# Made w2 sets in three tied parts from raw slots of their own, and probabilities transposed two positions later (tiles 9 to 17)

## The chip, the cores and the metric

One core of a Trainium2 chip runs the whole program in one launch. The metric is the device time of that core in microseconds. The kernel before took 1995.99 us, the median of three runs (1995.85 to 1996.73).

## The reference

Three layers follow one another. 2304 tokens of width 512 come out of an attention with a window of 64 keys; they go through a gated layer, and then through eight experts that all see every token and are added with weights from a normalisation of eight rounds.

```
scores = scale * q @ k.T ; masked to 0 <= rel < 64 ; softmax ; attn @ v     (4 x 8 heads, 576 x 64)
x = attn_out reshaped to 2304 x 512
x = (silu(x @ w_gate) * (x @ w_val)) @ w_out                                 (512 -> 1536 -> 512)
P = exp(x @ r_gate - max) ; 8 rounds of row and column normalisation         (2304 x 8)
out = sum over e of P[:, e] * (relu(x @ w1[e]) @ w2[e])                       (512 -> 1024 -> 512, e = 0..7)
```

## The kernel before, in words

The program has three stretches. First the attention of the first four tiles of 128 tokens. Then the gated layer, in five blocks of 4, 4, 4, 4 and 2 tiles, with the attention of the later tiles woven in. Last the experts. Products are made of a high and a low part of each operand, so each product is three passes: high by high, high by low, low by high.

The middle stretch is a list of events that is walked once (`ev`, `add`). Its unit is a position: twelve matmuls of 512 columns. Three positions make one hidden tile f of block b: "gv" kind 0 (gate, PSUM bank 4), "gv" kind 1 (value, bank 5) and "o" (the output product of the hidden tile before, banks 0 to 3). Position 3s+kind belongs to hidden tile s = 12b+f. Around these, the stages of attention tile t are put at p plus an offset, with p = 9(t-5) for t from 4 on (`STEPS`, `SHIFT`): transposes of q and k ("tqk", L297, banks 4 and 7), scores ("s", L320, banks 6 and 7, reduced by VectorE at L332), exponentials on ScalarE ("exp", L409), the normalisation on VectorE ("norm", L417 to L423), transposes of the probabilities ("t", L440, banks 6 and 7, copied out by ScalarE at L282 and VectorE at L284), and the product with v ("pv", L457, bank 6, copied out by ScalarE at L470 and VectorE at L473). At three positions after each block's end the router's logits of that block are made ("lg", L826, bank 6; copied at L841) and transposed ("lgt", L853, bank 7). A scheduler then sets each engine's order from these events; an engine works through its list in that order and does not pass over an instruction that waits.

ScalarE and VectorE also split weights into high and low parts. `split_1` does it for the gated layer (L605 on ScalarE, L606 on VectorE; from "saved" copies in DRAM). `split_w2q` makes one set of w2 of an expert: it reads two raw tiles, forms sums and differences (L700, L701, L715, L716), splits seven pieces (L675, L678 on ScalarE, L684, L687 on VectorE) into a staging buffer of seven tiles, and stores them in one DMA of 1792 KB (L731) for the experts' stretch. There are 20 such sets (experts 1 to 5, four each), two in every three hidden tiles from s = 12 on, each as one event.

All raw tiles, saved weights and w2 alike, come through one ring of slots (`o_raw` of six, and two more, `o_more`, in the middle stretch: `place_raws`), in the order in which they are used. A load is issued by SyncE when its slot's last reader is done (`load_one`, L560). All DMAs of the program are issued by SyncE, in one list.

Of the kernel before, what the change touches and what calls it, by code (L numbers as in the profile page):

```python
# [17 lines left out]
def attention_moe_moe2(  # L18
# [13 lines left out]
    nc = tc.nc  # L32
# [63 lines left out]
    o_ident = take("F", 128)  # L96
    o_ones = take("F", 128)
    o_mask = take("F", 3 * WK)
    o_logit = take("F", NTILE * NE)
    o_prob = take("F", NTILE * NE)  # L100
    o_rows = take("F", NTILE)
    o_cols = take("F", NE)
    o_part = take("F", NE)
    o_gmax = take("F", 2)
    o_stat = take("F", NSC * 3 * H)
    o_lgs = takes("F", 128, 6)
    o_wgp = take("F", KD * 32)
    NRAW = 6
# [11 lines left out]
    o_acc = takes("F", 512, 2 * HTT)  # L120
    o_more = o_acc[4:6]
    sizes["F"] = max(sizes["F"], f_top)
# [4 lines left out]
    o_qraw = takes("bF", 512, 3)  # L127
    o_kraw = takes("bF", 512, 3)
    o_xc = take("bR", 2 * 7 * 2 * HT)

# [16 lines left out]
    o_wc = [o_x[1], o_wr[4], o_x[0]]  # L147
    o_stw = [o_w2[0], o_w2[4]]

    o_last = take("R", 2 * HT)  # L150
# [56 lines left out]
    def emit_consts():  # L207
        make_identity(nc, ident)
        nc.vector.tensor_copy(sl(o_idr, 128, True), ident)
        m = sl(o_stage + 512, 192)  # L210
        nc.gpsimd.memset(m, 0.0)

        nc.gpsimd.affine_select(out=m, in_=m, pattern=[[1, 192]], compare_op=ALU.is_gt, fill=NEG, base=0, channel_multiplier=-1)
        nc.gpsimd.affine_select(out=m, in_=m, pattern=[[-1, 192]], compare_op=ALU.is_ge, fill=NEG, base=WIN, channel_multiplier=1)

        for i in range(3):
            for r, c, n in ((0, 64, 64), (0, 0, 64), (64, 64, WK)):
                rows = slice(r, r + 64)
# [8 lines left out]
        nc.gpsimd.memset(ones, 1.0)  # L227
        nc.gpsimd.memset(sl(o_wgp, KD * 32), 0.0)
# [290 lines left out]

    raw_at = []  # L520
    raw_prev = []
    raw_done = set()
    raw_held = set()

    def place_raws(ready):
        ring = o_raw + o_more
        last = {}
        for n in range(len(raw_keys)):
            if n < 2 * NCONV:
                o = o_raw[n % NRAW]  # L530
            elif n < ready:
                o = ring[(n - 2 * NCONV) % len(ring)]
            else:
                o = next(raw_at[i] for i in range(n - len(ring), n) if raw_at[i] in o_raw and last[raw_at[i]] == i)
            raw_at.append(o)
            raw_prev.append(last.get(o))
            last[o] = n

# [6 lines left out]
    def load_one():  # L545
        n = w_load[0]
        if n >= raw_stop[0] or n >= 2 * NCONV and raw_prev[n] is not None and raw_prev[n] not in raw_done:
            return False
        w_load[0] += 1
        key, i = raw_keys[n]  # L550
        src = sources(key)[i]
        if wide(key):
            dst = sl(o_wide[n % NWIDE], 1024).bitcast(I32)
        elif key[0] == "x":
            dst = sl(raw_at[n], HT)
        else:
            dst = sl(raw_at[n], 512)
# [50 lines left out]
    def raw_slots(key):  # L608
        cnt = sum(1 for r in raw_keys if r[0] == key)
        n = w_next[0]  # L610
        assert raw_keys[n][0] == key and w_load[0] >= n + cnt, (key, n, w_load)
        w_next[0] += cnt
        return [raw_at[n + i] for i in range(cnt)]

# [119 lines left out]

# [40 lines left out]
    def do_split(key):  # L775
        {"1": split_1, "w1": split_w1, "w2": split_w2, "w2q": split_w2q, "x": split_x}[key[0]](key)

# [80 lines left out]

    def emit_gmax1():
        nc.vector.tensor_reduce(sl(o_gmax, 1), logit, AX.X, ALU.max)  # L860
        nc.vector.tensor_copy(sl(o_lgs[0], 128), sl(o_gmax, 1).to_broadcast([128, 128]))
# [459 lines left out]
    def add(*e):  # L1321
        ev.append(e)
# [143 lines left out]
    }  # L1466
    made = [("w2q", e, 0, j) for e in range(1, NE - 2) for j in range(NF2 // 2)]
    seq = [(b, f) for b in range(NB) for f in range(NF1)]
    prev = None
    for s, (b, f) in enumerate(seq):  # L1470
        for kind in range(3):
# [12 lines left out]
            att_at(3 * s + kind)  # L1484
        if s == 1:
# [7 lines left out]
    assert not made  # L1493
    late = [("w1", 0, 0, 2), ("w2", 0, 0, 6), ("w1", 0, 0, 3), ("w2", 0, 0, 7)]
# [87 lines left out]

    raw_first = []
    for e in ev:
# [7 lines left out]
        elif e[0] == "w2h" and e[3] == 0:  # L1592
            key = ("w2q", e[1], 0, e[2])
        if e[0] == "w1n" and key is not None and not raw_first:
            raw_first.append(len(raw_keys))
        if key is not None:
            raw_keys.extend((key, i) for i in range(len(sources(key))))

    place_raws(raw_first[0])

# [21 lines left out]
    def banks(x):  # L1622
# [45 lines left out]
        "unlock": emit_unlock,  # L1668
        "w2h": emit_w2h,
        "w2r": emit_w2r,  # L1670
        "p": emit_p,
# [13 lines left out]
    for e in ev:  # L1685
# [6 lines left out]
        if e == ("gv", NB - 1, NF1 - 1, 1):  # L1692
            last_hid.update((ins.engine, ins) for ins in added[begin:])
        if e[0] == "w2h":
            for ins in added[begin:]:
                if ins.engine in (mybir.EngineType.DVE, mybir.EngineType.Activation):
                    tc.add_manual_dep(
# [44 lines left out]
```

## Time and profile before

| | |
|---|---|
| median of three runs | 1995.99 us |
| the profiled execution | 1994.68 us |
| its span, first to last instruction | 1992.9 us |
| TensorE (matmul) busy | 1965.0 us, 99% |
| VectorE busy | 1509.4 us, 76% |
| ScalarE busy | 1233.9 us, 62% |
| GpSimd busy | 41.2 us, 2% |
| DMA: moved, mean rate | 529.36 MB, 266 GB/s |

Busy time is the time in which an engine has an instruction of the program running. Matmuls overlap and their ends are modelled. A busy TensorE is one that has work, not one at its peak. What an engine waits for is inferred from the semaphores. The profiled execution took 1.8 us more than its span, which lies before the first and after the last instruction.

### The profile page before, as it was taken

To read this page: it belongs to the slowest core of one execution; us is meant where nothing else is said; L and a number is where in the kernel's file an instruction comes from. 1 tells how busy PE (TensorE), PEld (TensorE's weight loads), DVE (VectorE), ACT (ScalarE), POOL (GpSimd) and SP (SyncE) were. 2 spreads that over 40 slices of the span, in tenths; PEclk is the share of its full clock that TensorE was granted. 3 is DMA by queue.
4 is the path that set the end of the run, shared out by engine and by line. 5 is a ranking of instruction groups with operands and counts; after the bars stand their busy time and mean duration, and the time that the engine had idled before them with its cause. 6 is when DMAs were issued, how large, how long until landed. Compare 5 with 4: busy or idle time off the path is not lost.

```text
span 1992.9 us, 33648 instructions
## 1 busy us (share of the span) xinstructions
PE 1965.0 (99%) x11815; PEld 1855.9 (93%) x11815; DVE 1509.4 (76%) x3298; ACT 1233.9 (62%) x2795; POOL 41.2 (2%) x77
## 2 busy tenths in 40 slices
PE   8999999999999999999999999999999999999998
PEld 6887877778998999999999999999999999999998
DVE  7987777877677999989987777868777566666566
ACT  7766676766552677777764566657565455555555
POOL 3100000000000000000000000000000000000000
PEclk9999999999999999999999999999999999999999
DMA  9988889777764869979888889989877877777775
GB/s 243 280 271 253 247 230 290 240 242 222 230 225 166 302 212 296 369 244 342 264 287 268 262 301 325 333 301 333 289 248 267 279 260 261 261 260 246 268 240 170
DMA packets 303002, 529.36 MB, mean 266 GB/s; under 512 B 74976, under 2 KB 159728, under 8 KB 302320
## 3 DMA queue, kind: packets, MB, share of 16 engines
q1 hardware_dynamic: 302832, 527.21, 81.2%
q8 instruction: 93, 1.52, 0.3%
q14 instruction: 77, 0.63, 0.1%
HBM read 390.74 MB, written 136.39 MB: 265 GB/s over the span
## 4 chain that ended last, share of the span: by engine, by line
PE 91%; DVE 3%; DMA 3%; ACT 2%; issue 0%; SPq 0%; POOL 0%; DVEq 0%; ACTq 0%
PE ps L1138 34%; PE ps L1271 34%; PE ps L788 12%; PE ps L806 6%; DMA area_F<-in_moe_w_dram 2%; PE ps L965 2%; PE ps L919 2%; PE ps L457 1%; PE ps L440 1%; ACT area_bF L409 0%; PE ps L297 0%; PE ps L320 0%; PE ps L1301 0%; DVE area_R L606 0%; DVE area_bF L423 0%
## 5 line engine op out<-in xcount | busy, mean ns | idle before, releaser
L1138 PE MATMUL ps<-area_bR,area_R 128*128 128x384 f32 x3864 | 771.5, 335 | 0.0
L1271 PE MATMUL ps<-area_R 128*128 128x384 f32 x3864 | 770.6, 334 | 0.0
L1138 PEld LDWEIGHTS ps<-area_bR,area_R 128*128 128x128 f32 x3864 | 678.0, 188 | 1.6 <-ACT area_F L1306 0.3
L1271 PEld LDWEIGHTS ps<-area_R 128*128 128x128 f32 x3864 | 678.5, 188 | 0.0
L1196 DVE TENSOR_TENSOR area_R<-area_aG,area_R 128x384 fp32r<-128x384 f32 x637 | 350.9, 554 | 238.5 <-ACT area_R L1192 232.9
L1192 ACT CAST area_R<-area_aG 128x384 fp32r<-128x384 f32 x637 | 327.0, 514 | 306.3 <-PE ps L1271 256.0
L788 PE MATMUL ps<-area_R 128*128 128x512 f32 (+1 forms) x1068 | 234.8, 374 | 3.3 <-ACT area_F L793 3.3
L788 PEld LDWEIGHTS ps<-area_R 128*128 128x128 f32 x1068 | 188.2, 190 | 41.9 <-ACT area_F L793 3.9
L1261 ACT COPY area_SF<-ps 128x384 f32<-128x384 f32 x320 | 152.5, 478 | 86.8 <-PE ps L1271 84.3
L1170 DVE TENSOR_TENSOR area_aG<-area_aG 128x384 f32<-128x384 f32 x364 | 197.1, 552 | 4.3
L675 ACT CAST area_R<-area_F 128x256 fp32r<-128x256 f32 x284 | 115.4, 407 | 59.8 <-PE ps L1138 42.7
L1239 ACT COPY ps<-area_SF 128x384 f32<-128x384 f32 x280 | 135.4, 485 | 6.8 <-DVE area_SF L1265 2.6
L1148 DVE TENSOR_TENSOR area_F<-area_F,ps 128x384 f32<-128x384 f32 x184 | 101.1, 549 | 38.7 <-PE ps L1138 38.2
L684 DVE TENSOR_TENSOR area_R<-area_F,area_R 128x256 fp32r<-128x256 f32 x284 | 117.7, 416 | 12.3 <-ACT area_R L675 11.6
L806 PE MATMUL ps<-area_SR,area_R 128*128 128x512 f32 (+1 forms) x540 | 122.7, 376 | 0.2 <-ACT area_SR L797 0.2
L1150 ACT COPY area_F<-ps 128x384 f32<-128x384 f32 x184 | 88.4, 480 | 39.8 <-PE ps L1138 39.1
L1160 DVE SCALAR_TENSOR_TENSOR area_aG<-ps,area_F 128x384 f32<-128x384 f32 x182 | 100.6, 553 | 15.2 <-PE ps L1138 15.2
L806 PEld LDWEIGHTS ps<-area_SR,area_R 128*128 128x128 f32 x540 | 93.5, 190 | 18.4 <-issue 1.2
L1160 DVE SCALAR_TENSOR_TENSOR area_aG<-area_F 128x384 f32<-128x384 f32 x182 | 100.3, 551 | 1.3
L606 DVE TENSOR_TENSOR area_R<-area_F,area_R 128x512 fp32r<-128x512 f32 x108 | 74.3, 695 | 32.5 <-ACT area_R L605 20.6
L605 ACT CAST area_R<-area_F 128x512 fp32r<-128x512 f32 x108 | 65.9, 620 | 51.3 <-PE ps L788 17.6
L788 PE MATMUL ps<-area_R,area_SR 128*128 128x512 f32 (+1 forms) x372 | 81.5, 368 | 1.4 <-ACT area_R L470 1.4
(171 smaller groups left out, 1623.3 us busy)
## 6 DMA issues: line engine op xcount, KB each, us to landing
area_R<-w2p SPq DMA_DIRECT2D x322, 512.0 KB, 5.1
area_R<-w1p SPq DMA_DIRECT2D x182, 512.0 KB, 4.4
w1p<-area_R SPq DMA_DIRECT2D x98, 512.0 KB, 5.9
area_F<-in_moe_w_dram SPq DMA_DIRECT2D x160, 256.0 KB, 5.7
area_F<-saved SPq DMA_DIRECT2D x144, 256.0 KB, 4.7
w2p<-area_aR SPq DMA_DIRECT2D x20, 1792.0 KB, 9.2
w2p<-area_F SPq DMA_DIRECT2D x12, 1536.0 KB, 8.6
saved<-area_F SPq DMA_DIRECT2D x18, 512.0 KB, 6.9
```

Source lines behind the costliest of these rows:

```text
L675: nc.scalar.copy(as_r(sl(o, 256)), src)
L684: nc.vector.tensor_tensor(out=as_r(v[:, 256:512]), in0=src, in1=v[:, 0:256], op=ALU.subtract)
L788: nc.tensor.matmul(ps, lhsT=w3[:, kk, :], rhs=x3[:, kk, :], start=(i == 0), stop=(i == 3 * KD - 1))
L806: nc.tensor.matmul(PS[m][:, 0:n], lhsT=sl(o + 512 * wp + m * 128, 128, True), rhs=sl(oh + 512 * xp, n, True), start=(f == 0 and i == 0), s ...
L1138: nc.tensor.matmul(ps, lhsT=sl(o + wp * 256 + kk * 128, 128, True), rhs=sl(o_xc + xp * 14 * HT + (B_OF[m] * 2 + kk) * HT, HT, True), start ...
L1160: nc.vector.scalar_tensor_tensor(out=sl(o_c[at], HT), in0=c, scalar=0.0, in1=sl(o_p[k % 2][q_ % 2], HT), op0=ALU.max, op1=ALU.mult)
L1170: sub = lambda o, a, b: nc.vector.tensor_tensor(out=o, in0=a, in1=b, op=ALU.subtract)
L1192: nc.scalar.copy(sl(o, HT, True), src)
L1196: nc.vector.tensor_tensor(out=sl(o + HT, HT, True), in0=src, in1=sl(o, HT), op=ALU.subtract)
L1239: nc.scalar.copy(l2_bank(n, dt), macc(MSEQ[i], dt))
L1261: nc.scalar.copy(macc(m, dt), l2_bank(7 * k + i, dt))
L1271: nc.tensor.matmul(l2_bank(7 * k + i, dt), lhsT=sl(o + wp * 256 + dt * 128, 128, True), rhs=sl(jit_of[w] + hp * HT, HT, True), start=(j == ...
```

## The change

It has two parts.

The made sets of w2 leave the ring. They get two pairs of raw slots of their own, for even and odd sets (`o_qraw2`: the former `o_more`, and a new slot beside a reused one, `o_late`, in which the router's small buffers lie later). The ring has six slots throughout, and `place_raws` is gone. A set is now three events ("q", n, part) at positions 2, 3, 5 (even) and 6, 8, 9 (odd) of a period of nine positions, from position 36 on. Each part's instructions on VectorE, ScalarE and SyncE are tied to the order in which the events are written. Set n+2's raw loads are issued at the end of set n. The store of 1792 KB is five stores of 512, 256, 256, 256 and 512 KB, each issued with the next part.

For tiles t from 9 on, "t" moves from p+13 to p+15, and "pv" from p+16 to p+17 (to p+16 still, for the last tile of a block).

The constant `ones` is written later (at "gmax1"), since its place is now used for raw slots first.

```diff
-    o_more = o_acc[4:6]
+    o_spare = take("bF", 512)
+    o_qraw2 = [o_acc[4:6], [o_spare, o_late]]
+    QSETS = [(e, j) for e in range(1, NE - 2) for j in range(NF2 // 2)]
...
-        if n >= raw_stop[0] or n >= 2 * NCONV and raw_prev[n] is not None and raw_prev[n] not in raw_done:
+        if n >= raw_stop[0] or n >= 2 * NCONV and n - NRAW not in raw_done:
...
-    def split_w2q(key):
-        _, e, g, j = key
-        r = [sl(o, 512) for o in raw_slots(key)]
-        st = o_stw[(e * NF2 // 2 + j) % 2]
-        o = lambda m: st + 512 * MSEQ.index(m)
-        w2_first(r, o)
-        w2_second(r, o)
-        w2_third(r, o)
-        nc.sync.dma_start(out=kept(e, j), in_=sl(st, 7 * 512).rearrange("p (m w) -> p m w", m=7))
-        load_w()
-        load_w()
+    def q_set(n):
+        e, j = QSETS[n]
+        r = [sl(o, 512) for o in o_qraw2[n % 2]]
+        return e, j, r, o_stw[n % 2], lambda m: o_stw[n % 2] + 512 * MSEQ.index(m)
+
+    def emit_qload(n):
+        if n < len(QSETS):
+            e, j, r, st, o = q_set(n)
+            for dst, src in zip(r, w2_sources(e, j)):
+                nc.sync.dma_start(out=dst, in_=src)
+
+    def emit_qstore(n, part):
+        if 0 <= n < len(QSETS):
...
+            for i, k in ((5, 2),) if part == 0 else ((0, 1), (2, 1)) if part == 1 else ((1, 1), (3, 2)):
+                nc.sync.dma_start(out=v[:, i:i + k, :], in_=at(i, k))
+
+    def emit_q(n, part):
+        e, j, r, st, o = q_set(n)
+        if part == 0:
+            emit_qstore(n - 1, 2)
+            w2_first(r, o)
+        elif part == 1:
+            emit_qstore(n, 0)
+            w2_second(r, o)
+        else:
+            emit_qstore(n, 1)
+            w2_third(r, o)
+            emit_qload(n + 2)
...
+        if t > 2 * BT[0]:
+            at = at[:6] + (15, 16 if t % BT[0] == BT[0] - 1 else 17)
...
-    made = [("w2q", e, 0, j) for e in range(1, NE - 2) for j in range(NF2 // 2)]
+    sets_at = {}
+    for n in range(len(QSETS)):
+        for part, i in enumerate(((2, 3, 5), (6, 8, 9))[n % 2]):
+            sets_at.setdefault(3 * NF1 + 9 * (n // 2) + i, []).append(("q", n, part))
+    sets_at.setdefault(3 * NF1 - 3, []).append(("qload", 0))
+    sets_at.setdefault(3 * NF1, []).append(("qload", 1))
...
-        if s >= NF1 and s % 3 < 2 and made and (b, f) < (NB - 2, 9):
-            add("split", made.pop(0))
```

Lines of the changed program have other numbers: L792 and L810 are "gv" and "o" (L788 and L806 before), L590 is L606, L668 and L671 are L684 and L687, L684 and L685 are L700 and L701, L799 and L802 are the hidden tile's L795 and L798, L544 is L560; L716 is a set's own raw load and L724 its store.

On TensorE, around the transposes of tile 12's probabilities (L440; "gv" writes banks 72 and 73, "o" 68 to 71, L297 the next tile's transposes). Before:

```order
L806 MATMUL ps_71<-area_SR,area_R 128x512 x3
L788 MATMUL ps_72<-area_R 128x512 x12
L788 MATMUL ps_73<-area_R 128x512 x12
L440 MATMUL ps_74<-area_F,area_bF 128x128 x4
L440 MATMUL ps_75<-area_F,area_bF 128x128 x4
L806 MATMUL ps_68<-area_SR,area_R 128x512 x3
L806 MATMUL ps_69<-area_SR,area_R 128x512 x3
L806 MATMUL ps_70<-area_SR,area_R 128x512 x3
L806 MATMUL ps_71<-area_SR,area_R 128x512 x3
L788 MATMUL ps_72<-area_R 128x512 x12
L788 MATMUL ps_73<-area_R 128x512 x12
L297 MATMUL ps_72<-area_F,area_bF 128x128 x4
```

The same place now:

```order
L792 MATMUL ps_73<-area_R 128x512 x12
L810 MATMUL ps_68<-area_SR,area_R 128x512 x3
L810 MATMUL ps_69<-area_SR,area_R 128x512 x3
L810 MATMUL ps_70<-area_SR,area_R 128x512 x3
L810 MATMUL ps_71<-area_SR,area_R 128x512 x3
L792 MATMUL ps_72<-area_R 128x512 x12
L440 MATMUL ps_74<-area_F,area_bF 128x128 x4
L440 MATMUL ps_75<-area_F,area_bF 128x128 x4
L792 MATMUL ps_73<-area_R 128x512 x12
L297 MATMUL ps_72<-area_F,area_bF 128x128 x4
L297 MATMUL ps_75<-area_F,area_bF 128x128 x4
```

The transposes stand 24 matmuls later, behind the next "o" and the next gate product; one value product is left between them and the next tile's transposes. Further on, "pv" stands behind the "o" that it stood ahead of.

On VectorE, from the splits ahead of tile 12's scores to their reduction (L332). Before:

```order
L606 TENSOR_TENSOR area_SR<-area_F,area_SR 128x512
L687 TENSOR_TENSOR area_aR<-area_F,area_aR 128x2x256
L700 TENSOR_TENSOR area_F<-area_F 128x256
L795 TENSOR_TENSOR area_F<-area_F,ps_73 128x512
L701 TENSOR_TENSOR area_F<-area_F 128x256
L684 TENSOR_TENSOR area_aR<-area_F,area_aR 128x256
L715 TENSOR_TENSOR area_F<-area_F 128x256
L798 TENSOR_TENSOR area_SR<-area_F,area_SR 128x512
L332 ISA area_bF,area_F<-ps_74,area_F 128x128
```

The same place now:

```order
L590 TENSOR_TENSOR area_SR<-area_F,area_SR 128x512
L671 TENSOR_TENSOR area_aR<-area_F,area_aR 128x2x256
L684 TENSOR_TENSOR area_F<-area_F 128x256
L685 TENSOR_TENSOR area_F<-area_F 128x256
L799 TENSOR_TENSOR area_F<-area_F,ps_73 128x512
L590 TENSOR_TENSOR area_SR<-area_F,area_SR 128x512
L668 TENSOR_TENSOR area_aR<-area_F,area_aR 128x256
L802 TENSOR_TENSOR area_SR<-area_F,area_SR 128x512
L332 ISA area_bF,area_F<-ps_74,area_F 128x128
```

The first part of a set (its L687, now L671) still stands ahead of the reduction; the third part's L715 does not.

In SyncE's list of DMAs, around the loads of tile 13 (in_moe_w_dram are raw tiles of w2, w2p the made sets). Before:

```order
L731 DMA w2p<-area_aR 896x1x512
L560 DMA area_F<-in_moe_w_dram 128x512
L560 DMA area_F<-saved 128x512
L560 DMA area_F<-in_moe_w_dram 128x512
L253 DMA area_F<-in_v_dram 64x8x64 x2
L560 DMA area_F<-saved 128x512
L253 DMA area_bF<-in_k_dram 128x8x64
L253 DMA area_bF<-in_q_dram 128x8x64
L560 DMA area_F<-saved 128x512 x2
```

The same place now:

```order
L724 DMA w2p<-area_aR 128x512 x2
L716 DMA area_bF<-in_moe_w_dram 128x512
L716 DMA area_F<-in_moe_w_dram 128x512
L544 DMA area_F<-saved 128x512
L724 DMA w2p<-area_aR 128x512
L724 DMA w2p<-area_aR 128x2x512
L544 DMA area_F<-saved 128x512
L724 DMA w2p<-area_aR 128x2x512
L253 DMA area_bF<-in_k_dram 128x8x64
L253 DMA area_bF<-in_q_dram 128x8x64
```

A load now stands behind a store of 768 KB at most, where it stood behind one of 1792 KB; the list has 1280 entries in place of 1200.

## Rows read from the trace of the kernel before

**Rows 1.** Windows: stretch, length, busy PE PEld DVE ACT POOL, clock, DMA share, GB/s

```profile
150.00:570.00 420.00, 406.18 (x2622) 336.83 (x2621) 306.61 (x739) 273.29 (x615) 17.51 (x27) 1.00 0.79 244
570.00:1950.00 1380.00, 1379.98 (x7930) 1369.41 (x7929) 1050.32 (x2313) 831.77 (x1892) 0.00 (x0) 1.00 0.82 275
```

**Rows 2.** Waits of PE in 150:570: total us, times, longest us

```profile
PE ps L440 <- DVE area_bF L423: 8.4, 5, 3.5
PE ps L853 <- DVE area_F L332: 3.1, 2, 1.7
PE ps L297 <- ACT area_F L793: 1.1, 2, 0.6
PE ps L320 <- DVE area_F L841: 0.9, 1, 0.9
```

**Rows 3.** Timeline of PE, tile 12: start, us, instructions, [idle before, releaser]

```profile
294.57 1.06 PE L440 MATMUL ps<-area_F,area_bF 128*128 128x128 f32 x8 [3.53 <-DVE area_bF L423]
...
298.22 1.07 PE L788 MATMUL ps<-area_R 128*128 128x512 f32 x4
```

**Rows 4.** Timeline of ACT in the same stretch

```profile
283.78 0.62 ACT L678 CAST area_aR<-area_F 128x512 fp32r<-128x512 f32 x1 [4.23 <-DMA area_F<-in_moe_w_dram]
```

**Rows 5.** Timeline of DVE in the same stretch

```profile
284.43 0.69 DVE L687 TENSOR_TENSOR area_aR<-area_F,area_aR 128x512 fp32r<-128x512 f32 x1 [4.79 <-ACT area_aR L678]
...
293.19 1.23 DVE L423 TENSOR_TENSOR area_bF<-area_bF,area_F 128x1024 f32<-128x1024 f32 x1
...
296.12 0.69 DVE L284 COPY area_bF<-ps 128x512 f32<-128x512 f32 x1
```

**Rows 6.** Waits of ACT in 150:570

```profile
ACT area_aR L678 <- DMA area_F<-in_moe_w_dram: 18.7, 11, 4.2
```

**Rows 7.** DMA issues in 150:570: count, KB each, median us to landing

```profile
w2p<-area_aR SPq DMA_DIRECT2D x20, 1792.0 KB, 9.2
area_F<-saved SPq DMA_DIRECT2D x133, 256.0 KB, 4.9
area_F<-in_moe_w_dram SPq DMA_DIRECT2D x56, 256.0 KB, 4.6
...
w1p<-area_R SPq DMA_DIRECT2D x4, 256.0 KB, 3.0
```

**Rows 8.** Timeline of PE, tile 16

```profile
419.14 1.94 PE L440 MATMUL ps<-area_F,area_bF 128*128 128x128 f32 x8 [2.85 <-DVE area_bF L423]
...
424.42 1.75 PE L788 MATMUL ps<-area_R 128*128 128x512 f32 x7
```

**Rows 9.** Windows, as rows 1, of that place

```profile
419.10:422.52 3.42, 3.38 (x12) 3.09 (x13) 2.26 (x4) 3.39 (x7) 0.00 (x0) 0.50 0.71 257
```

**Rows 10.** Timeline of PE, tile 12's "pv" to tile 13's scores

```profile
304.63 1.15 PE L457 MATMUL ps<-area_bF,area_F 128*64 128x64 f32 x32
...
315.35 1.10 PE L320 MATMUL ps<-area_F,area_bF 64*64 64x128 f32 x32
316.38 3.06 PE L806 MATMUL ps<-area_SR 128*128 128x512 f32 x12
...
321.09 0.66 PE L853 MATMUL ps<-area_F 128*128 128x128 f32 x4 [1.43 <-DVE area_F L332]
```

**Rows 11.** Timeline of DVE in the same stretch

```profile
308.49 0.68 DVE L473 TENSOR_TENSOR area_R<-ps,area_R 128x512 fp32r<-128x512 f32 x1
...
316.44 0.43 DVE L684 TENSOR_TENSOR area_aR<-area_F,area_aR 128x256 fp32r<-128x256 f32 x1 [2.96 <-ACT area_aR L675]
316.78 0.68 DVE L795 TENSOR_TENSOR area_F<-area_F,ps 128x512 f32<-128x512 f32 x1
...
319.26 0.28 DVE L332 CUSTOM_DVE_ANT_0 area_bF<-ps,area_F 128x128 f32<-128x128 f32 x1
```

**Rows 12.** DMA issues in 505:565, the last block

```profile
area_F<-saved SPq DMA_DIRECT2D x25, 256.0 KB, 3.8
area_F<-in_moe_w_dram SPq DMA_DIRECT2D x16, 256.0 KB, 3.2
```

More of the change, by code (lines that the diff above doesn't have):

```diff
@@ L96, in attention_moe_moe2 @@
     o_ident = take("F", 128)
-    o_ones = take("F", 128)
+    o_late = take("F", 512)
+    o_prob, o_rows, o_ones = o_late, o_late + NTILE * NE, o_late + HT
+    o_cols = o_rows + NTILE
+    o_part = o_cols + NE
+    o_gmax = o_part + NE
     o_mask = take("F", 3 * WK)
     o_logit = take("F", NTILE * NE)
[L100 to L104, printed above, removed]
     o_stat = take("F", NSC * 3 * H)
+    o_wgp = take("F", KD * 32 + 16)
     o_lgs = takes("F", 128, 6)
-    o_wgp = take("F", KD * 32)
     NRAW = 6
@@ L226, in emit_consts @@
         nc.gpsimd.tensor_copy(sl(o_maskr + 2 * WK, WK, True), sl(o_mask + 2 * WK, WK))
-        nc.gpsimd.memset(ones, 1.0)
         nc.gpsimd.memset(sl(o_wgp, KD * 32), 0.0)
@@ L518, in attention_moe_moe2 @@
     w_next = [0]
-    raw_at = []
-    raw_prev = []
     raw_done = set()
     raw_held = set()
[L525 to L537, printed above, removed]
     def load_w():
@@ L554, in load_one @@
         elif key[0] == "x":
-            dst = sl(raw_at[n], HT)
+            dst = sl(o_raw[n % NRAW], HT)
         else:
-            dst = sl(raw_at[n], 512)
+            dst = sl(o_raw[n % NRAW], 512)
         if len(src.shape) == 3:
@@ L612, in raw_slots @@
         w_next[0] += cnt
-        return [raw_at[n + i] for i in range(cnt)]
+        return [o_raw[(n + i) % NRAW] for i in range(cnt)]
     def wr_slot(kind, b, f):
@@ L721, in w2_third @@
         piece_lo(a12, o(3))
[L723 to L733 removed]
+    def q_set(n):
[10 more added lines that the diff above has]
+            e, j, r, st, o = q_set(n)
+            at = lambda i, k, d=1: sl(st + 512 * i, 512 * (k * d)).rearrange("p (k m w) -> p k m w", m=d, w=512)[:, :, 0]
+            v = kept(e, j)
+            for i, k in ((5, 2),) if part == 0 else ((0, 1), (2, 1)) if part == 1 else ((1, 1), (3, 2)):
+                nc.sync.dma_start(out=v[:, i:i + k, :], in_=at(i, k))
+    def emit_q(n, part):
+        e, j, r, st, o = q_set(n)
+        if part == 0:
[8 more added lines that the diff above has]
+            emit_qload(n + 2)
     ORDER2 = (1, 2, 6, 5, 7, 3, 4)
@@ L775, in do_split @@
     def do_split(key):
-        {"1": split_1, "w1": split_w1, "w2": split_w2, "w2q": split_w2q, "x": split_x}[key[0]](key)
+        {"1": split_1, "w1": split_w1, "w2": split_w2, "x": split_x}[key[0]](key)
     def emit_gv(b, f, kind):
@@ L859, in emit_gmax1 @@
     def emit_gmax1():
+        nc.gpsimd.memset(ones, 1.0)
         nc.vector.tensor_reduce(sl(o_gmax, 1), logit, AX.X, ALU.max)
@@ L1466, in attention_moe_moe2 @@
     }
-    made = [("w2q", e, 0, j) for e in range(1, NE - 2) for j in range(NF2 // 2)]
+    sets_at = {}
[4 more added lines that the diff above has]
+    sets_at.setdefault(3 * NF1, []).append(("qload", 1))
+    last_set = max(sets_at) + 1
+    sets_at[last_set] = [("qstore", len(QSETS) - 1, 2)]
     seq = [(b, f) for b in range(NB) for f in range(NF1)]
@@ L1484, in attention_moe_moe2 @@
             att_at(3 * s + kind)
+            for e in sets_at.pop(3 * s + kind, []):
+                add(*e)
         if s == 1:
@@ L1488, in attention_moe_moe2 @@
             add("split", key)
-        if s >= NF1 and s % 3 < 2 and made and (b, f) < (NB - 2, 9):
-            add("split", made.pop(0))
         prev = (b, f)
-    assert not made
+    assert not sets_at
     late = [("w1", 0, 0, 2), ("w2", 0, 0, 6), ("w1", 0, 0, 3), ("w2", 0, 0, 7)]
@@ L1593, in attention_moe_moe2 @@
             key = ("w2q", e[1], 0, e[2])
-        if e[0] == "w1n" and key is not None and not raw_first:
-            raw_first.append(len(raw_keys))
         if key is not None:
             raw_keys.extend((key, i) for i in range(len(sources(key))))
-    place_raws(raw_first[0])
     marked = []
@@ L1669, in attention_moe_moe2 @@
         "w2h": emit_w2h,
+        "q": emit_q,
+        "qload": emit_qload,
+        "qstore": emit_qstore,
         "w2r": emit_w2r,
@@ L1693, in attention_moe_moe2 @@
             last_hid.update((ins.engine, ins) for ins in added[begin:])
-        if e[0] == "w2h":
+        if e[0] in ("w2h", "q"):
+            engines = [mybir.EngineType.DVE, mybir.EngineType.Activation]
+            if e[0] == "q":
+                engines.append(mybir.EngineType.SP)
             for ins in added[begin:]:
-                if ins.engine in (mybir.EngineType.DVE, mybir.EngineType.Activation):
+                if ins.engine in engines:
                     tc.add_manual_dep(
```

1 line of the change is left out of this document (removed).

## The prediction

> **What bounds the kernel now.** I read the windows first, because they say where a change to the gated layer can be worth anything. In [rows 1] the reader is to compare a stretch's length with its busy TensorE. The experts' stretch, 570 to 1950, has TensorE busy for 1379.98 of 1380.00 us: nothing that VectorE, ScalarE or the DMAs do there is seen in the time. The stretch that the change touches, 150 to 570, has 406.18 of 420.00 busy. So 13.8 us of idle TensorE are there to be had, and a half clock, told below. VectorE is busy for 306.61 and ScalarE for 273.29 of these 420, so neither bounds by its sum: what TensorE waits for are single late results in lists that are worked through in order.
>
> The waits of TensorE name them [rows 2]: 8.4 us in five waits at the transposes of the probabilities (L440) for the last step of "norm" (L423), 3.1 us in two waits of the logits' transposes (L853) for the scores' reduction (L332), and 1.1 us in two at the q and k transposes (L297) for the gate product's bank (L793). I then followed the longest, tile 12, back through the timelines of three engines. TensorE was at L440 3.53 us too early [rows 3]. L423 started at 293.19 and took 1.23. At the other end of that chain VectorE had stood for 4.79 us ahead of L687, which waited for ScalarE's L678 [rows 5], and L678 had stood 4.23 us for a raw tile of w2 [rows 4]. The views agree on the root: the loads are late, and a late load holds VectorE's list with "norm" in it. It is no single accident, since ScalarE waits so 18.7 us in eleven places [rows 6]. Why the loads are late is in the DMA view: the whole set's store takes 9.2 us to land, and loads in the same stretch take 4.6 and 4.9 [rows 7], where in the last block, which stores no set, they take 3.2 and 3.8 [rows 12].
>
> **The sum, part by part.** It is made against the profiled execution, 1994.68 us (span 1992.9 and 1.8 around it); the median of the runs is 1.31 above that.
>
> *The transposes two positions later.* No TensorE instruction is added or taken away. "T" stands 24 matmuls of 512 columns later. Between the end of the transposes (295.63) and 298.22 twelve such matmuls ran [rows 3], 2.59 us; another row of twelve spans 3.06 from its first to its last [rows 10]. So 24 take 5.2 to 6.1, and I take 5.4. The worst lateness was 3.5 [rows 2]. Even if VectorE is as late as before, every one of the five is covered with at least 1.7 us to spare: **-8.4**.
>
> *The clock.* At tile 16 the wait was 2.85 us, and after it the granted clock was 0.50, the lower of the two levels [rows 9]. From the start of the transposes to the gate product there took 5.28 us (419.14 to 424.42, [rows 8]); the same work at tile 12 took 3.65 at full clock (294.57 to 298.22, [rows 3]). Without the wait the clock should stay: **-1.6**. The bounds are 0 (it falls all the same) and -1.6.
>
> *The q and k transposes.* They used to follow "gv" directly. Now the probabilities' transposes (1.06 us, [rows 3]) stand between the gate product and the value product ahead of them, so they come due about a microsecond later, while the longest wait was 0.6 [rows 2]: **-1.1**.
>
> *The logits' transposes.* Their wait comes from the list of VectorE: at tile 13 it stood 2.96 us ahead of L684 for a late split of w2, so L795 began at 316.78 and L332 at 319.26, though the scores had begun at 315.35 [rows 10, 11]. That split is not in the list ahead of it any more (the order of VectorE), so L795 can begin about when the scores do, and L332 2.48 us behind it as before. From L332's first row to the logits' transposes, which waited for its last, 1.83 us passed (319.26 to 321.09). So they could start 4.3 us after the scores' start. They now stand right behind "o", which ended at 319.44 [rows 10], and so are due 4.1 us after it. I leave 0.4 us at each of three places, 1.2, where the 3.1 stood and the 0.9 of the scores (L320) that waited for the logits' copy behind them [rows 2]: **-2.8**. Bounds: -4.0 (no wait left) and +0.3 (all three as long as the 1.43 of tile 13).
>
> *"Pv" and the logits.* At the end of blocks the logits' product now has one product of 2.7 us between it and "pv", and its bank is emptied by L473. That ended 4.54 us after "pv" began at tile 12 (304.63 to 309.17, [rows 10, 11]), 3.4 after "pv" ended. That is 0.7 late at worst, and nothing where VectorE isn't held up: **+0.4**, bounds 0 and 1.8. The bank that the next transposes of q and k write is emptied by L284, which ended 1.2 us after the probabilities' transposes (296.81 against 295.63, [rows 5, 3]); one value product of 2.7 lies between. Nothing.
>
> *The made sets.* The instructions on ScalarE and VectorE are the same ones, 20 sets of seven pieces. What moves is when their loads are issued: at the end of the set two before, in place of behind the ring. A set comes every 4.5 positions of 2.7 us, 12.2 us, so a load has about that long where it lands in 4.6 [rows 7]. Then L678's 4.23 and VectorE's 4.79 go. TensorE has nothing more to gain from it than is counted above, but it is what keeps the sum from depending on the 24 matmuls alone. New here are ties: each part's DVE, ACT and SP instructions stand in the written order. Behind a part's first DVE instruction, if its load is late, wait "norm", L795 and L332; behind a store that waits for a split, all later loads. I allow **+2** for such waits, from nothing (loads in time) to 6 (a quarter of an L678 wait of 4.2 at each of six tiles).
>
> *The ring of six.* The last block loads 41 tiles of "saved" and w2 in 60 us [rows 12], one per 1.5 us. With a landing of 3.8 and a split of 0.62 and 0.69 on two engines [rows 4, 5], a slot turns round in 5.1 us, so six slots give one per 0.85 and eight one per 0.64. Enough on the mean; bursts may find it empty: **+0.5**, bounds 0 and 5.
>
> Together: -8.4 - 1.6 - 1.1 - 2.8 + 0.4 + 2 + 0.5 = -11.0. 1994.7 - 11.0 = 1983.7 in the terms of the profile, and 1.3 for the median of the runs: **1985.0**. That leaves about 3 us of the 13.8 idle.
>
> **The rivals.** *The waits move.* In-order lists hold what is left: the first part of a set still stands ahead of L332, the logits wait at three tiles, the half clock begins after some other wait. If the logits' transposes give nothing (0), the clock stays (0), the logits' product waits 1.8 and the ties and the ring take 4: -8.4 - 1.1 + 5.8 = -3.7, about 1992; with half of these 1989. For it: three of the five terms hang on VectorE's list. Against: the largest hangs on distance alone.
>
> *Nothing to be measured.* The ring's burst (5) and the ties (6) come in full: -13.7 + 0.4 + 11 = -2.3, 1993.7. What this kernel's measurement can tell from no change is about 0.2%, 4 us, so this would be within it. For it: ScalarE's wait list shows that loads decide, and the ring loses two slots of eight. Against: the ring loses the sets' loads as well.
>
> *Slower: five pieces of a store cost more than one.* The store has 14 KB a partition in one transfer; now five transfers. A small lone one took 3.0 us to land [rows 7]. In series five take 15 us, more than the 12.2 between sets; each set would then run 2.8 us behind the last, and 20 of them 56 us: 2052. It decides from 2.4 us a piece in series. Against it: 213 transfers of [rows 7] lie in 420 us, one per 2.0 us, while they take 3 to 9 each, so transfers overlap here.
> The Trainium skill, "DMA: Bandwidth & Descriptors", has rules against this part of the change: its section "Rules for kernel authors" tells to merge small transfers into large ones, and "Anatomy of one DMA" gives a fixed 2.0 us and the bytes at 436 GB/s. By that fit, an estimate, one store takes 6.2 us and five pieces 14.2 if nothing overlaps. The trace disagrees with the first figure (9.2 us, [rows 7]: the store shares the queues with loads), and no row of before shows pieces of a set.
>
> **How the numbers follow.** The forecast has 0.68, waits that move 0.16, nothing 0.10, slower 0.06 (most of it this last mechanism, or one of its kind at a smaller price). The forecast's own range is 1981 (nothing for the ties, the ring and the logits' waits) to 1988.5 (half of the logits' term not won, ties at 4). The range of 8 in 10 goes from 1980.5 up to 1991.8, which takes in most of the second case and leaves out the third and fourth. Faster by over 0.2% (under 1992.0): 0.84; within: 0.10; slower: 0.06.
>
> **What would show it.** Right: in the new profile no wait of TensorE at L440 for L423; no wait at the q and k transposes for L793; waits of 0.3 to 0.5 us at the logits' transposes; full clock behind tile 16's transposes; ScalarE's waits for raw w2 gone; the store's pieces landing well under 9.2 us and the loads nearer 3 than 4.9. Wrong: TensorE waiting at L440 still, or at "pv" or the logits' product for L473; waits for "saved" in the last block that reach TensorE; a half clock elsewhere in 150 to 570; pieces that land one behind the other.

## The result, and the profile after

The changed kernel took 1977.57 us, the median of four runs (1977.17 to 1978.55), against 1996.36 for the kernel before: a ratio of 0.9904, with a 95% interval from 0.9892 to 0.9917. Forecast were 1985.0 and a range from 1980.5 to 1991.8. The sign was right. The time came out 7.4 us under the forecast and 2.9 under the range. The profiled execution took 1977.46 us (span 1975.7), 17.2 less than that of before. One execution among the runs below, the profiled one of e14, took 5150.83 us; it is left out of e14's number, and e14 has no trace to read.

The windows of the changed kernel, which answer to [rows 1] (the second one ends where the last 43 us begin, in both):

```profile
150.00:570.00 420.00, 419.24 (x2700) 350.58 (x2697) 321.17 (x780) 281.55 (x633) 21.44 (x28) 1.00 0.79 253
570.00:1932.70 1362.70, 1362.68 (x7830) 1353.56 (x7829) 1034.75 (x2270) 821.56 (x1871) 0.00 (x0) 1.00 0.82 275
```

Of 13.8 us of idle TensorE 0.8 are left, at full clock. The waits of TensorE in that stretch, which answer to [rows 2], are one line:

```profile
PE ps L792 <- DVE area_F L799: 0.8, 1, 0.8
```

The place of [rows 3] and [rows 5], tile 12, on TensorE and then on VectorE:

```profile
276.16 1.10 PE L320 MATMUL ps<-area_F,area_bF 64*64 64x128 f32 x32
...
290.97 1.04 PE L440 MATMUL ps<-area_F,area_bF 128*128 128x128 f32 x8
```

```profile
274.21 0.69 DVE L671 TENSOR_TENSOR area_aR<-area_F,area_aR 128x512 fp32r<-128x512 f32 x1
...
282.22 0.17 DVE L417 TENSOR_SCALAR area_F<-area_F 128x8 f32<-128x8 f32 x1 [1.63 <-ACT area_bF L409]
282.66 1.23 DVE L423 TENSOR_TENSOR area_bF<-area_bF,area_F 128x1024 f32<-128x1024 f32 x1
```

L671, which was L687, has no idle time ahead of it where it had 4.79 us. The normalisation ends at 283.89, 7.7 us after the start of the scores, where it ended 12.9 after it before. The transposes start 14.8 us after the scores. They have 7.1 us to spare, and the old position, 9.5 us after the scores, would have been late enough too. That is the first hint that the forecast's largest term stood in the wrong place.

The DMA issues in the same stretch (count, KB each, median us to landing), against [rows 7]:

```profile
area_F<-saved SPq DMA_DIRECT2D x133, 256.0 KB, 3.8
w2p<-area_aR SPq DMA_DIRECT2D x40, 512.0 KB, 5.9
w2p<-area_aR SPq DMA_DIRECT2D x60, 256.0 KB, 3.6
area_F<-in_moe_w_dram SPq DMA_DIRECT2D x49, 256.0 KB, 4.3
```

The five pieces of a store land in medians of 3.6 and 5.9 us and overlap. The rival that had them one behind the other fell.

Where the 17.2 us of the two profiled executions went can be read from when the same gate products start in both. At 60 us the changed kernel is 1.05 ahead, at the last gate product 16.75, at the end 17.2. The middle 15.7 are the ten waits of before that lie ahead of the last gate product (13.4, less the 0.8 left), the half clock of [rows 8, 9] (1.6), and 0.16 us at each wait that the waits' list does not count: at tile 12 the first transpose started 3.92 us after the matmul ahead of it, of which 3.53 is the wait, where 0.23 is usual. Ten of these less the one left are 1.4. By this count the middle comes to 15.6. An eleventh wait, of 0.16, stands behind the last gate product.

### The profile page after: what moved, and what is told of

Same layout as the page of the kernel before. It is cut to its first block, busy times and chain, and to the rows that moved or that the text cites. A ratio compares the mean times of both kernels' runs of the same rounds, so it can differ in the third digit from the quotient of the medians.

```text
span 1975.7 us, 33881 instructions
## 1 busy us (share of the span) xinstructions
PE 1961.1 (99%) x11815; PEld 1854.1 (94%) x11815; DVE 1508.1 (76%) x3298; ACT 1233.2 (62%) x2795; POOL 46.8 (2%) x77
## 4 chain that ended last, share of the span: by engine, by line
PE 97%; ACT 1%; DVE 1%; DMA 0%; issue 0%; SPq 0%; DVEq 0%; ACTq 0%
PE ps L1143 34%; PE ps L1276 34%; PE ps L792 14%; PE ps L810 7%; PE ps L970 2%; PE ps L924 2%; PE ps L457 1%; PE ps L440 1%; PE ps L320 1%; PE ps L297 0%; ACT area_bF L402 0%; PE ps L1306 0%; DVE area_F L566 0%; DVE area_F L573 0%; PE ps L830 0%; DMA area_aF<-in_moe_w_val_dram 0%
## 5 line engine op out<-in xcount | busy, mean ns | idle before, releaser
L792 PE MATMUL ps<-area_R 128*128 128x512 f32 (+1 forms) x1068 | 236.0, 374 | 4.0 <-ACT area_F L797 3.3
L792 PEld LDWEIGHTS ps<-area_R 128*128 128x128 f32 x1068 | 186.3, 190 | 42.2 <-ACT area_F L797 3.7
L668 DVE TENSOR_TENSOR area_R<-area_F,area_R 128x256 fp32r<-128x256 f32 x284 | 118.2, 418 | 9.4 <-ACT area_R L659 8.9
L810 PE MATMUL ps<-area_SR,area_R 128*128 128x512 f32 (+1 forms) x540 | 120.7, 372 | 0.0
L810 PEld LDWEIGHTS ps<-area_SR,area_R 128*128 128x128 f32 x540 | 93.5, 189 | 17.7 <-issue 1.2
L590 DVE TENSOR_TENSOR area_R<-area_F,area_R 128x512 fp32r<-128x512 f32 x108 | 74.6, 695 | 36.8 <-ACT area_R L589 29.5
L792 PE MATMUL ps<-area_R,area_SR 128*128 128x512 f32 (+1 forms) x372 | 81.8, 369 | 1.3 <-ACT area_R L470 1.3
```

Source lines behind the costliest of these rows:

```text
L668: nc.vector.tensor_tensor(out=as_r(v[:, 256:512]), in0=src, in1=v[:, 0:256], op=ALU.subtract)
L792: nc.tensor.matmul(ps, lhsT=w3[:, kk, :], rhs=x3[:, kk, :], start=(i == 0), stop=(i == 3 * KD - 1))
L810: nc.tensor.matmul(PS[m][:, 0:n], lhsT=sl(o + 512 * wp + m * 128, 128, True), rhs=sl(oh + 512 * xp, n, True), start=(f == 0 and i == 0), s ...
```

## The experiments

Each was timed in five rounds beside the kernel before, whose medians lay between 1992.41 and 1994.09 in these sessions; ratios are to that kernel, in the same session. The changed kernel was not timed again in them. Against a kernel before of 1992 to 1994, its 1977.57 would be a gain of 15 to 16.5 us. In what follows, the lead of a load is the time from its issue to its use, and its landing the time from its issue until the data are there.

**The two parts apart.** The first kernel is the one before with the transposes' new positions alone; the second is the changed kernel without them.

```
# e1: before, with
+        if t > 2 * BT[0]:
+            at = at[:6] + (15, 16 if t % BT[0] == BT[0] - 1 else 17)
# e2: changed, with
-        if t > 2 * BT[0]:
-            at = at[:6] + (15, 16 if t % BT[0] == BT[0] - 1 else 17)
```

> The kernel before with the probabilities' transposes (and pv) of tiles 9 to 17 later, and nothing else. Theory A (late raw tiles of w2 are the root, both parts remove the same waits at the transposes): L440's waits (8.3 us in 6 places, and 0.16 us of restart behind each), the half clock at tile 16 (1.6) and the waits at L297 (1.1) go, those at L320 and L853 (3.9) stay, ScalarE still waits some 35 us for raw w2; about 1984 us, between 1982 and 1986. Theory B (the 24 matmuls of distance are the whole gain, the sets' part gives nothing): all of the gain, 1977 to 1979.

> The changed kernel with the transposes put back to their old positions, so only the made sets are changed. In the changed kernel the normalisation ends 7.7 to 8.4 us after the start of a tile's scores, where it ended 8.0 to 12.9 after it before, and the old position of the transposes is due 9.5 us after it. Theory A (late raw tiles are the root): no wait at L440, L853 or L320 is left, and the time is that of the changed kernel, 1977 to 1980 us. Theory B (distance): waits of 1 to 3 us at L440 stay, with a half clock after one of them, 1986 to 1990 us.

Measured: e1 1988.47 us, 0.9976 (0.9967 to 0.9986); e2 1977.29 us, 0.9923 (0.9910 to 0.9937). The sets' part gives everything, 16.1 us; the positions give 4.9 when they are alone and nothing beside it. That is theory A, but e1 won less than A had said. Its longest waits of TensorE tell why:

```profile
PE ps L806 <- ACT area_F L816: 2.2, 1, 2.2
PE ps L853 <- DVE area_F L332: 1.8, 2, 1.2
PE ps L788 <- ACT area_F L793: 0.9, 1, 0.9
PE ps L788 <- DVE area_R L473: 0.6, 1, 0.6
PE ps L297 <- DVE area_bF L284: 0.6, 2, 0.3
```

No wait at L440 is left, as the forecast had it (five of 8.4 us in [rows 2]; the 8.3 in six places above is a slip). ScalarE still waits for raw w2 and for "saved", though, and what stands behind those waits in its list and VectorE's is late for somebody else: the copy of the output product, silu, the copy of "pv".

**What of the sets' part counts.** e3 stores each set whole, e4 drops SyncE's tie (the other engines' lists are then the same word for word), e8 keeps nothing but the own slots and the early loads.

```
# e3: changed, in emit_qstore
+            if part == 2:
+                nc.sync.dma_start(out=v, in_=at(0, 7))
# e4: changed, with
-                engines.append(mybir.EngineType.SP)
# e8: e2, one untied event per set where it was before
+        w2_first(r, o)
+        w2_second(r, o)
+        w2_third(r, o)
+        nc.sync.dma_start(out=kept(e, j), in_=sl(st, 7 * 512)...)
+        emit_qload(n + 2)
```

> The changed kernel, with each set stored whole (1792 KB in one DMA) behind its third part, in place of five pieces. Theory A1 (it counts that the raw tiles are loaded a set ahead, not how the store is cut): loads behind a store land in 5 to 10 us again but are needed 12 us or more later; 1977 to 1980 us. Theory A2 (the smaller stores are what brings the loads in time, saved weights in the ring above all): saved's median landing goes from 3.8 back to about 4.9 us, ScalarE waits for saved, TensorE waits 3 to 6 us; 1982 to 1985 us.

> The changed kernel without the tie of the sets' DMAs to SyncE's written order; the order of every other engine is the same. Theory A1 (a load a set ahead has time enough, wherever it stands in SyncE's list): 1977 to 1980 us. Rival (the tie is what keeps stores that wait for a split from standing ahead of loads): loads are issued later, ScalarE waits for raw tiles or saved, 1981 to 1986 us.

> Own raw slots and loads two sets ahead, and nothing else of the change: each set is one untied event behind its hidden tile as before, its store whole, the transposes in their old places. Theory A (late raw tiles are the whole root): 1977 to 1980 us. Rival C (the cut and the ties): the set's 13 instructions on VectorE stand in a block ahead of the scores' reduction, waits at L440 and L853 stay, 1985 to 1992 us.

Measured: e3 1977.31 us, 0.9925 (0.9911 to 0.9939); e4 1977.92, 0.9923 (0.9909 to 0.9936); e8 1977.66, 0.9923 (0.9910 to 0.9936). All three are the changed kernel's time. With the loads two sets ahead, neither the cut, nor the ties, nor the small stores are needed. In e8 the whole store lands in a median of 8.9 us, and TensorE has two waits left in 150 to 570, 0.8 us at the logits and 0.5 at a gate or value product.

**The lead taken away, in doses.** e6 and e7 load a set's raw tiles at the end of the set just before, one to two positions ahead of use; e11 three positions ahead, where e2 has six.

```
# e6 (from e2) and e7 (from the changed kernel)
-            emit_qload(n + 2)
+            emit_qload(n + 1)
# e11 (from e2): the loads as events of their own
+            sets_at.setdefault(3 * NF1 + 9 * (n // 2) + (-1, 3)[n % 2], []).append(("qload", n))
```

> e2 (new sets, transposes in their old places), with each set's raw tiles loaded at the end of the set before instead of two sets before: one position (some 2.7 us) ahead of use for the odd sets, two for the even ones, where a load lands in 3.7 us. Theory A (late raw tiles in an in-order list are the root): ScalarE and VectorE wait 1 to 2 us at the first part of the odd sets, the normalisation loses its 1.65 us of slack at some tiles, waits at L440, L853 or L320 come back, 1979 to 1986 us. Rival C (the cut into three parts and their ties is what counts, the loads' time isn't): no wait of TensorE, 1977 to 1978 us.

> The changed kernel with the same late loads as e6. Theory A: the same waits on ScalarE and VectorE, but the transposes two positions later have 7 us of slack and don't wait; what is left are waits at L853 and the scores, 1977 to 1981 us, below e6. If the two positions are worth nothing even then: the same time as e6.

> e2 (new sets, transposes in their old places) with the raw loads issued three positions (some 8 us) ahead of use, between e2's six and e6's one to two. A load lands in about 4 us. Theory A: enough, ScalarE doesn't wait for raw w2, 1977 to 1979 us. If the lead counts beyond the landing (a load waits behind stores in SyncE's list): 1980 to 1990 us.

Measured: e6 1998.19 us, 1.0027 (1.0015 to 1.0039); e7 1996.20, 1.0015 (1.0004 to 1.0025); e11 1978.83, 0.9921 (0.9907 to 0.9934). Late loads cost all of the gain and more, beyond what A had said, with stores in five pieces, cut and tied sets, and in e7 the later transposes too. The longest waits of TensorE in e6 and then in e7 follow. These two executions are no typical ones: that of e6 took 2005.30 us, the second longest of twelve, and that of e7 1989.82, the shortest of twelve. (L857 is the logits' transposes, L820 the copy of the output product.)

```profile
PE ps L440 <- DVE area_bF L423: 15.9, 6, 4.9
PE ps L857 <- DVE area_F L332: 4.1, 2, 3.5
```

```profile
PE ps L792 <- ACT area_F L797: 4.0, 3, 1.7
PE ps L857 <- DVE area_F L332: 2.9, 3, 1.7
PE ps L810 <- ACT area_F L820: 1.3, 1, 1.3
```

The two positions again take away the waits at L440, and the late list shows up in smaller waits at other readers. In time they are worth little: the medians are 2.0 us apart, the intervals overlap, and that is the outcome that was to stand for "worth nothing even then". Three positions (some 8 us, for loads that land in 4) are enough.

**The sets in the ring.** e9 cuts and ties the sets but leaves their raw tiles in the ring; e10 is the kernel before with one more slot in its ring in the middle stretch; e13 is the kernel before with five small stores.

```
# e9: before, the set's slots held from its first to its third part
+            raw_held.update((at, at + 1))
+        (w2_first, w2_second, w2_third)[part](r, o)
# e10: before, with
-    o_more = o_acc[4:6]
+    o_more = [*o_acc[4:6], o_late]
# e13: before, in split_w2q
-        nc.sync.dma_start(out=kept(e, j), in_=sl(st, 7 * 512)...)
+        for i, k in ((5, 2), (0, 1), (2, 1), (1, 1), (3, 2)):
+            nc.sync.dma_start(out=kept(e, j)[:, i:i + k, :], in_=sl(st + 512 * i, 512 * k)...)
```

> The kernel before with its sets cut into three tied parts at the new positions, but its raw tiles still in the ring of eight, the store whole, the transposes in their old places. Theory A: ScalarE still waits some 20 to 35 us for raw w2, TensorE waits at L440 and L853, 1986 to 1994 us. Rival C (the cut and the ties are the gain): 1977 to 1980 us.

> The kernel before with one more slot in its ring for the middle stretch (nine; the ring of six in the last block, as in the changed kernel), nothing else. Rival D (the changed kernel gains only because it has more slots, ten in place of eight): a load comes one slot sooner, about half of the gain, 1983 to 1988 us. Theory A (a set's raw tiles have to come out of a queue that doesn't wait for the saved weights' readers, and two sets ahead): the loads stay behind readers in the common order, ScalarE still waits over 20 us for loads, 1987 to 1994 us.

> The kernel before with each set's store of 1792 KB issued as five DMAs (512, 256, 256, 256, 512 KB) at the same place, the end of the set; raw tiles stay in the ring of eight, sets and transposes where they were. Theory A (a load is late because it is issued when the set's last split frees its slot, not because of the size of the store ahead of it; the same 1792 KB stand ahead of it, in five): 1988 to 1996 us, ScalarE waits some 30 us for raw w2 and saved. Rival E (the one large store is what makes the loads behind it land 8 to 10 us late): loads land in 4 to 6 us, 1980 to 1986 us. The fifth rival of the forecast (pieces in series): over 2000 us.

Measured: e9 1988.91 us, 0.9977 (0.9968 to 0.9987); e10 1983.48, 0.9944 (0.9931 to 0.9956); e13 1977.65, 0.9924 (0.9911 to 0.9936). In e9 the normalisation is late as before, though ScalarE now waits less for raw w2 (18.7 us in [rows 6]) and more for "saved" (12.5 us before):

```profile
PE ps L440 <- DVE area_bF L423: 9.0, 6, 4.0
ACT area_R L605 <- DMA area_F<-saved: 20.4, 10, 4.2
ACT area_aR L678 <- DMA area_F<-in_moe_w_dram: 5.3, 4, 2.7
```

That is not what theory A had said of raw w2. The edit also holds a set's slots from its first part to its third, so e9 shows that the cut and the ties don't give the gain in the ring; that they aren't needed for it is shown by e8. One slot more is over half of the gain, which is rival D's figure. And the small stores alone are all of it: theory A's expectation for e13 was 10 us too high at its lower end, and rival E's still 2.4. TensorE's only wait in e13, and the issues of the pieces and of raw w2, all in 150 to 570:

```profile
PE ps L807 <- ACT area_SR L798: 0.3, 1, 0.3
```

```profile
w2p<-area_aR SPq DMA_DIRECT2D x39, 512.0 KB, 3.9
area_F<-in_moe_w_dram SPq DMA_DIRECT2D x60, 256.0 KB, 3.8
```

The pieces did not stay together at the end of the set, as the expectation had it. In the trace they leave as their splits end, a set's first and last 8.5 to 18.1 us apart, so a load stands behind a piece or two and not behind 1792 KB. So there are two edits, each enough by itself, early loads and small stores. A cause that explains both was wanted, and so was an answer to a doubt: the edit of the stores also changed VectorE's and ScalarE's lists, since these are ordered by when things are taken to be ready.

**Lists or loads.** Three kernels with the lists of TensorE, VectorE and ScalarE held, instruction for instruction, in those of another kernel; SyncE's is left free.

```
# at the end of the walk over the events
+        for x, y in zip(order, order[1:]):
+            tc.add_manual_dep(mine[y], mine[x].name, ...)    # order: that of the other kernel
# e14: stores of e13, order of before    e15: stores of before, order of e13
# e16: loads of e6, order of e2 (and e11)
```

> The small stores of e13 with the lists of TensorE, VectorE and ScalarE held, instruction for instruction, in the order of the kernel before. If the loads' landing is the cause: raw w2 lands in about 4 us, its waits mostly go, the normalisation ends at most 9.5 us after the scores' start at most tiles, 1977 to 1983 us. If the order of the lists is the cause: 1987 to 1995 us.

> The kernel before, its whole stores and its ring, with the lists of TensorE, VectorE and ScalarE held in the order of e13. If the loads' landing is the cause: loads behind a store land in 8 to 10 us still, VectorE waits in the list, 1987 to 1998 us. If the order of the lists is the cause: 1976 to 1980 us.

> e6 (raw tiles loaded one to two positions ahead of use) with the lists of TensorE, VectorE and ScalarE held in the order of e2, which e11 (three positions ahead) has too. If a late load in a list is enough by itself: waits at the transposes and the scores as in e6, 1988 to 2000 us. If it was the other order in e6 that cost: 1977 to 1981 us.

Measured: e14 1978.13 us (the median of five), 0.9923 (0.9909 to 0.9936); e15 2024.47, 1.0151 (1.0135 to 1.0166); e16 2066.07, 1.0358 (1.0342 to 1.0375). e15 and e16 lie above what either case had allowed, by 26 and 66 us. With the same lists, the stores decide (e14 against before, e15 against e13), and so does the lead of the loads (e16 against e11, 87 us). The order of the lists is no part of the gain of the small stores. The other way round it matters: lists made for loads that come in time lose most when they don't. ScalarE's largest wait for a load in e15 and in e16, where [rows 6] has 18.7 us (L681 is L678 of the kernel before, L665 is L662 of the changed one):

```profile
ACT area_aR L681 <- DMA area_F<-in_moe_w_dram: 56.8, 15, 7.9
```

```profile
ACT area_aR L665 <- DMA area_F<-in_moe_w_dram: 110.3, 18, 7.9
```

**Better versions.** With the middle full, TensorE's longest wait is the one of 3.3 us at the third gate product, near 44 us. Silu stands there behind the exponentials of tile 4 in ScalarE's list. e12 is e2 with these later, e17 is e13 with the same.

```
# e12 (from e2) and e17 (from e13)
-        4: (1, 7, 2, 6, 6, 7, 13, 14),
+        4: (1, 7, 2, 6, 10, 11, 16, 17),
```

> e2 with tile 4's exponentials and what follows them put later (positions 1, 2, 7 and 8 in place of -3, -2, 4 and 5). In e2 and the changed kernel TensorE's longest wait is 3.25 us at the third gate product for ScalarE's silu, which stands behind the eight exponentials of tile 4 (2.9 us) and a table load of 1.28; the clock falls to half behind it in some runs. If silu comes first this wait goes: 1973 to 1975 us. If a second table load and the later tile take it back elsewhere: 1977 us or more.

> The kernel before with five small stores per set (e13) and tile 4's exponentials later (e12), nothing else: the two smallest edits that gave something. If their gains add: 1973 to 1976 us, that of e12. If e13 is closer to the edge than e12's sets with loads ahead: 1976 to 1980 us.

Measured: e12 1974.82 us, 0.9905 (0.9890 to 0.9920); e17 1974.78, 0.9908 (0.9894 to 0.9921). Both runs of four lie between 1974.5 and 1976.9, the lowest medians of all. e17 reaches that with two edits to the kernel before, without the new slots, parts and ties. Waits of TensorE of 0.9 us and more in total in the whole of e12:

```profile
PE ps L240 <- DVE area_F L238: 1.5, 1, 1.5
PE ps L792 <- ACT area_R L470: 1.3, 1, 1.3
PE ps L383 <- DVE area_bF L365: 0.9, 2, 0.7
```

## Why the forecast was wrong

**The cause it named was right.** Raw tiles of w2 came late and held in-order lists with the normalisation in them. It put their lateness down to the landing alone (4.6 and 4.9 us in the medians of [rows 7], 3.2 and 3.8 in [rows 12]). What it didn't see is how short the lead was, and which loads stood behind the store. SyncE's waits in the kernel before say it (total us, times, longest):

```profile
SPq L560 <- DVE area_aR L684: 84.8, 26, 9.6
```

And SyncE's list at tile 12 of the kernel before (start, us to issue):

```profile
266.25 0.32 SPq L560 DMA_DIRECT2D area_F<-saved  x1
271.85 0.33 SPq L560 DMA_DIRECT2D area_F<-in_moe_w_dram  x1
272.45 0.32 SPq L560 DMA_DIRECT2D area_F<-saved  x1
272.87 0.53 SPq L731 DMA_DIRECT2D w2p<-area_aR  x1
273.44 0.65 SPq L560 DMA_DIRECT2D area_F<-in_moe_w_dram  x1
```

A load in the ring can't be issued before the last splits of a set (L684) free its slot, and the same splits release the whole set's store. So store and load go out together, 0.57 us apart; the load landed 10.3 us later, and L678 began at 283.78, when it had [rows 4]. For comparison SyncE's list in the changed kernel, for the set whose L671 is shown above:

```profile
260.16 0.33 SPq L716 DMA_DIRECT2D area_F<-in_moe_w_dram  x1
260.76 0.32 SPq L544 DMA_DIRECT2D area_F<-saved  x1
261.18 0.39 SPq L716 DMA_DIRECT2D area_F<-in_moe_w_dram  x1
```

It is loaded 13 us ahead. Tile 12 is no single case. Counted over 150 to 570 from the issues and landings in the traces, 15 of the 56 loads of raw w2 in the kernel before are issued within 2.5 us behind a whole store, and land in a median of 9.2 us; the other 41 land in 3.5. In e13, 20 of 60 are issued so behind a piece, and land in 4.4. In e10 two stand so behind a whole store, and in e3 and e8 none does. A list waits where the landing is longer than the lead. Early loads lengthen the lead (e8, e11), and small stores shorten the landing (e13; e14, with the old lists, takes the same time). A slot more lets a load go sooner, and hardly any stands behind a store then (e10). e6 and e7 wait in spite of small stores, since their lead is down to one or two positions of 2.7 us.

**Term by term.** *Transposes, -8.4:* the waits at L440 went, as said, and distance alone does that (e1). But it was credited to the wrong edit. In e2 and e8 they go without it; and where loads are late it only hands the lateness on, for a net 4.9 us in e1 where three terms that hung on it, 8.4, 1.6 and 1.1, were added up. This step failed: a wait at one reader was taken for the loss itself, while the loss was the list being late.

*The made sets, +2, with "TensorE has nothing more to gain from it than is counted above":* this is the step that put the forecast off, and it was the opposite. No tie was felt (e4 and e8, with fewer or none, have the same time), and this part alone has the whole gain (e2). With it went all that was left standing elsewhere: the logits' 1.2 and the 0.4 behind "pv" measured 0. These three terms make 3.6 of the 6.2 us between the sum of -11.0 and the profiles' -17.2.

*The clock, -1.6:* right; 150 to 570 is at 1.00. *The transposes of q and k, -1.1:* right. *The ring of six, +0.5:* the 0.8 left, about 0.9 with the 0.16 beside it, in the last block; mis-sized by 0.4 the other way.

*Not in the sum:* the 0.16 us at each of eleven waits, 1.8; and 1.05 at the start. These and the median below are why the time lies under the range: with every term at its better bound the sum is no more than -15.1, which gives 1980.9. The windows from 44 to 50 us of before, of the changed kernel and of e2, in this order, show where the 1.05 comes from:

```profile
44.00:50.00 6.00, 5.49 (x14) 4.22 (x14) 6.00 (x8) 3.90 (x5) 3.03 (x2) 0.50 1.13 329
```

```profile
44.00:50.00 6.00, 5.24 (x17) 4.19 (x18) 6.00 (x9) 4.76 (x7) 3.34 (x2) 0.72 1.12 351
```

```profile
44.00:50.00 6.00, 6.00 (x27) 4.77 (x28) 6.00 (x7) 3.99 (x5) 2.25 (x2) 1.00 1.08 358
```

The clock column reads 0.50, 0.72 and 1.00 behind the same wait of 3.3 us. This looks like a difference between executions and not of the kernels: over the first 50 us e1, whose start is that of the kernel before, has 0.97, where the trace of before has 0.94. e12 takes most of the wait away, and has 1.00 there.

*The median:* 1.3 us were added since the runs of before lay that much above its profile. Those of the changed kernel lie 0.1 above theirs: 1.2 of the 7.4.

**The rivals.** In the sum of "nothing" the first four terms are -13.9 and not -13.7, so that its case is 1993.5 and not 1993.7; no chance hangs on it. "The waits move" is what e1 and e7 show, for a kernel whose loads stay late; the changed kernel had none left to move. "Nothing" fell. "Slower" fell with e13, where the small pieces are the whole gain: the Trainium skill, "DMA: Bandwidth & Descriptors" ("Rules for kernel authors"), counsels one large transfer for many small, with the warning "under 64 KB you're paying mostly overhead"; the pieces here have 256 and 512 KB. In this stretch the smaller ones win, since the loads issued behind the large one pay for it: 10.3 us at tile 12, where loads of raw w2 that don't stand behind a store have a median of 3.5. The other section of that page of the Trainium skill that the forecast drew on, "Anatomy of one DMA", gives its fit for transfers issued by GpSimd, and all of this kernel's are issued by SyncE, so the 9.2 us of [rows 7] is no test of it. In e13 a set's last piece lands 3.3 us behind its issue in the median, where the whole store takes 9.2.

What stays open: how much of e13's gain is the size of a piece, and how much is that a piece leaves as soon as it is split. The two were not tried apart. Why the kernel before varies as it does is not shown either: its seventeen runs in one session spread over 8.2 us, six of e13 over 6.3, four of the changed kernel over 1.4. And early loads with the lists of before, the one corner missing from the crossing of lists and loads, was not tried.

## What to carry to other kernels

When an in-order engine is late, find the first thing in its list that waited, and cure that; moving the reader that complained makes room for one reader, and here left lateness to others. A ring of buffers whose loads are released by the same instructions as a large store gives the loads behind it the longest landing at the shortest lead; here either early loads or smaller stores were enough. An edit that changes a wait may change a scheduler's lists as well, so hold the lists before crediting either.

## What the hardware showed that was not expected

A wait of TensorE takes 0.16 us more than its listed length: at each of the ten in 150 to 568 of the trace of before, the starts of the matmuls ahead of it and behind it are 0.39 us and the wait apart, where 0.23 is usual without one. The list counts a wait from the end of the matmul ahead, and these ends are modelled, so the difference may be one of counting. A half clock follows a wait in some executions only: behind the 2.85 us of tile 16 and not the 3.53 of tile 12 in the same trace, and behind the 3.3 us near 44 us the clock over the window from 44 to 50 was 1.00, 0.72 and 0.50 in three executions.
